# Row statistics of a pair split into an early mean and late squares, a row tile turned earlier, and the last statistics spread over the mixing

## The chip, the cores and the metric

The kernel runs on one core of a Trainium2 chip. A core has five engines that each take their instructions in order and wait for each other through semaphores: TensorE (PE in the profile, its weight loads PEld), VectorE (DVE), ScalarE (ACT), GpSimd (POOL) and SyncE (SP, which only issues DMAs here). ScalarE and GpSimd issue DMAs too, and such an issue stands in the engine's own order. Data lies in HBM, in the core's SBUF, and in eight PSUM banks into which TensorE writes. The metric is the device time of one execution in microseconds.

## The reference

Two layers, each a linear attention block (A) and a gated block (B), on one sequence of 2048 rows of 512 features, in float32:

```python
x = x + A(layernorm(x)); x = x + B(layernorm(x))      # twice

def A(x):      # 32 heads of 16
    q, k, v = split(x @ wqkv)
    pq, pk = phi(q), phi(k)                           # phi(t) = where(t > 0, t + 1, exp(t)) + 1e-6
    kv, z = sum over rows of pk (x) v, sum over rows of pk
    return ((pq @ kv) / (pq @ z + 1e-6)) @ wo

def B(x):
    z = gelu(x @ w_in)                                # 2048 x 1792
    z1, z2 = z[:, :896], layernorm(z[:, 896:])
    g = w_sp @ z2 + b_sp[:, None]                     # w_sp is 2048 x 2048: the mixing
    return (z1 * g) @ w_out
```

The change concerns how `z2`, the normalised second half, is made in the second layer.

## The kernel before, in words

Every float32 product is made of three single-pass products: both factors are split into a high part (`fp32r`, by a copy on ScalarE) and a low part (the difference, by VectorE), and TensorE adds high x high, high x low and low x high. Everything on the small engines serves these splits, the statistics and the passing out of PSUM.

The order is written out by hand: each engine runs its instructions in the order in which the program calls them, and there is no scheduler. SBUF pages, larger tiles (`quads`, `bigs`) and PSUM banks come from lists in which the one that has been free longest is taken first, so a moved call also changes which buffer follows which.

A layer has four stages: `P1` (keys, queries), a transition, `P2` (output of the attention, then both halves of `gelu(x @ w_in)`), and `P4` (mixing, gate and output product). In `P2`, step `s` works on several row tiles of 128 rows at once:

- `b_high(s)`, `b_low(s)`: tile `s` of the attention's numerators, turned by way of DRAM, is transposed in blocks by VectorE (L353) and split on ScalarE and VectorE;
- `a2_den`, `a2_mul`: denominators of tile `s + 2`;
- `c(s-1)`: twelve matmuls (L117 to L119); `c2` adds the result to `x`; `c_stats` takes mean and variance on VectorE (L289, L291) and the inverse root on GpSimd (L293 to L296); `c3` normalises on ScalarE (L302) and stores the tile on SyncE's queue, from which `xturn.load` fetches it back turned once that store has landed;
- `d_high(s-2)`, `d_low(s-2)`: the tile normalised one step before is transposed (L353), its high part made by ScalarE (L103, into a `qd` tile), its low part by VectorE (L106);
- `f()`: one front unit, twelve matmuls for a piece of `z1`, a gelu on ScalarE (L996) and its store, issued on ScalarE's queue (L999).

In the second layer, from step 9 on, `z2` is made for pairs of row tiles. A pair `m` (tiles `2m` and `2m+1`) is a 2 x 2 block matrix that is multiplied by a 2 x 2 block weight with seven block products, P1 to P7, in place of eight (`product`, L805 to L807). They accumulate in PSUM: the bank `X` takes P1, then P6, then P7, then P4; the bank `Z` takes P5, then P3; `y` takes P2. Between them ScalarE copies a bank into the tile of `z` (`copy`, L824) and VectorE adds another one to it (`add`, L819). `block_sums` forms sums of the blocks (L766 to L769), which `parts` splits for P3, P5, P6 and P7 (written into tiles named `z_s` or into pages). A pair lasts three steps: an odd step makes P1 and P2 of pair `m` and P7, P4 and P3 of the pair before (`o`); an even step makes P6 and P5 of pair `m`; the last quarter of pair `m` is added and passed through gelu in the even step of pair `m + 1`.

Each gelu (`gelu`, L814) also leaves the sum of its rows. `row_stats` turns the two sums of a row tile into the negative mean `nm` on GpSimd (L831), takes the sum of squared deviations with two ScalarE instructions (L836, which write into a PSUM bank that nobody reads), and finds `rs` and `nb` on GpSimd (L840 to L843). `e4` then normalises the tile on ScalarE (L302), and for the first eight tiles subtracts two column ranges on VectorE (L975).

The order in an odd step, cut to what matters: `b`, `a2_den`, `c`, P7 and its copy, P1 and its copy, P2, `c2`, `c_stats`, the addition of `Z` to tile `2o+1`'s high half, `a2_mul`, `c3`, two gelus, `f`, `d`, `block_sums`, P4 and its gelu, P3, `parts`, `f`, `e4` of pair `m - 2`. P3 writes into the bank `Z` that the addition reads. In an even step: `b`, last quarter of pair `m - 1`, `a2_den`, `c`, `c2`, `c_stats`, `a2_mul`, `parts`, `f`, `c3`, P6 and a copy, P5, `row_stats` of pair `m - 1`, `d`, `f`.

The mixing `P4` also uses seven products, of 8 steps each; a mixing step `g` is `mm(g)`, 24 matmuls on eight banks (L1239 to L1241), behind `prepare`, which splits weights of step `g + 2` (L1198, L1205) and rows of step `g + 3` (L1203, L1209). Before the loop, the remaining front units run, and `finish` ends the last pair: last quarter, row statistics and normalisation, in one piece.

Of the kernel before, what the change touches and what calls it, by code (L numbers as in the profile page):

```python
# [10 lines left out]
F32 = mybir.dt.float32  # L11
F32R = mybir.dt.float32r
AF = mybir.ActivationFunctionType
OP = mybir.AluOpType

P = 128
S = 2048
D = 512
FH = 896
# [35 lines left out]
def mixer_kernel(ctx: ExitStack, tc: tile.TileContext, x_in, wqkv, wo_d, win1_d, win2_d, wsp_d, bsp_d, wout_d,  # L55
                 ident_d, mask_d, out_d):
    nc = tc.nc
    consts = ctx.enter_context(tc.tile_pool(name="consts", bufs=1))
    main = ctx.enter_context(tc.tile_pool(name="main", bufs=1))
    small = ctx.enter_context(tc.tile_pool(name="small", bufs=4))  # L60
# [70 lines left out]
    class Weight:  # L131


        def __init__(self, slots, shape, pieces, turned=False, keep=None):
            self.slots, self.shape, self.pieces, self.turned, self.keep = slots, shape, pieces, turned, keep
            self.h = self.l = None
            self.raw = deque()
            self.n_load = self.n_split = 0
# [139 lines left out]
    def w_in1():  # L278
        return Weight(bigs, [P, NF, 4, P], [win1_d[f] for f in range(NF)], keep=kept_in1)
# [358 lines left out]
    class P2:  # L638
        def __init__(self, p1):
            self.L = L = p1.L  # L640
            self.p1 = p1
            self.win1, self.win2 = (w_in1() if self.L == 0 else Parts(kept_in1, NCHK, 3)), p1.win2
            self.qturn, self.xturn = Turn(f"qt{L}", range(5), True), Turn(f"yt{L}", range(4))
            self.qp, self.qT, self.x, self.ms, self.xB, self.z, self.zms = {}, {}, {}, {}, {}, {}, {}
            self.fq = deque()
            self.fnext = []
            self.rows = []
            self.S, self.S_pages = [None, None], []
            self.X, self.Z, self.acc = {}, {}, {}
            self.sums2 = None if self.L == 0 else Sums2()  # L650

        def loadx(self, i):
# [170 lines left out]
                ztag(i, [P, FH], f"z{self.L}")  # L823
            nc.scalar.activation(ztile[i][:, s], b, AF.Copy)  # L824

        def row_stats(self, i):

            a, b = self.acc.pop(i)
            k = FH ** -0.5
            nm = small.tile([P, 1], F32, name="nm")  # L830
            nc.gpsimd.tensor_scalar(nm, a, b, -k / FH, op0=OP.add, op1=OP.mult)  # L831
            sq = banks.get([P, HF])
            v = []
            for s in (self.LO, self.HI):
                w = small.tile([P, 1], F32, name="sq", tag=f"sq{s.start}")
                nc.scalar.activation(sq, ztile[i][:, s], AF.Square, bias=nm, scale=k, accum_out=w)  # L836
                v.append(w)
            banks.put(sq)
            rs = small.tile([P, 1], F32, name="rs")
            nc.gpsimd.tensor_scalar(rs, v[0], v[1], LN_EPS, op0=OP.add, op1=OP.add)  # L840
            nc.gpsimd.tensor_tensor(rs, rs, mhalf, op=OP.pow)
            nb = small.tile([P, 1], F32, name="nb")
            nc.gpsimd.tensor_scalar(nb, nm, rs, 1 / k, op0=OP.mult, op1=OP.mult)  # L843
            self.zms[i] = None, rs, nb
# [14 lines left out]
        def odd(self, s):  # L859

            m = (s - 3) // 2
            o = m - 1
            new, old = m < HT, o >= PAIRED
            if s < NT:
                self.b_high(s)
                self.b_low(s)
            self.a2_den(s + 2)
            if s <= NT:
                self.c(s - 1)
            if old:  # L870
                self.product(self.X[o], o, "P7")
                self.copy(2 * o + 1, self.HI, self.X[o])
            if new:
                X, y = banks.get([P, HF]), banks.get([P, HF])
                self.X[m] = X
                self.product(X, m, "P1", start=True)
                self.copy(2 * m, self.LO, X)
                self.product(y, m, "P2", start=True, stop=True)
            if s <= NT:
                self.c2(s - 1)  # L880
                self.c_stats(s - 1)
            if old:
                self.add(2 * o + 1, self.HI, self.Z[o])
            self.a2_mul(s + 2)
            if s <= NT:
                self.c3(s - 1)
                self.xturn.load(s - 1)
            self.a(s + 3)
            if old:
                self.gelu(2 * o + 1, self.HI)  # L890
            if new:
                self.add(2 * m, self.LO, y)
                banks.put(y)
                self.gelu(2 * m, self.LO)
            self.f()
            if new:
                self.d_high(s - 2)
                self.d_low(s - 2)
                self.block_sums(m)
            if old:  # L900
                X = self.X.pop(o)
                self.product(X, o, "P4", stop=True)
                self.gelu(2 * o + 1, self.LO, X)
                banks.put(X)
                self.product(self.Z[o], o, "P3", stop=True)
                pages.put(*self.S_pages)
                self.S_pages = []
            if new:
                self.S[0] = self.parts(self.sraw[0], (2 * m + 1, 2 * m + 2))
            self.f()  # L910
            self.two(self.e4, m - 2)

        def even(self, s):

            m = (s - 4) // 2
            if s < NT:
                self.b_high(s)
                self.b_low(s)
            self.last_quarter(m - 1)
            self.a2_den(s + 2)  # L920
            if s <= NT:
                self.c(s - 1)
                self.c2(s - 1)
                self.c_stats(s - 1)
            self.a2_mul(s + 2)
            self.S[1] = self.parts(self.sraw[1], (2 * m + 5, 2 * m + 6))
            self.f()
            if s <= NT:
                self.c3(s - 1)
                self.xturn.load(s - 1)  # L930
            self.a(s + 3)
            Z = self.Z[m] = banks.get([P, HF])
            self.product(self.X[m], m, "P6")
            self.copy(2 * m, self.HI, self.X[m], False)
            self.product(Z, m, "P5", start=True)
            self.two(self.row_stats, m - 1)
            if s <= NT + 1:
                self.d_high(s - 2)
                self.d_low(s - 2)
            self.f()  # L940

        def finish(self):
            m = HT - 1
            self.last_quarter(m)
            self.two(self.row_stats, m)
            self.two(self.e4, m)

        def e(self, i):
            n, k = divmod(i, 4)
# [187 lines left out]
    class P4:  # L1137
# [203 lines left out]
        def run(self, nxt):  # L1341
            p2 = self.p2
            self.prepare(0, 0)
            self.fetch(2)
            while p2.f():
                pass
            if p2.L == 0:
                p2.win1.free()
            self.prepare(1, 1)
            self.fetch(3)  # L1350
            self.prepare(None, 2)
            if p2.L > 0:
                p2.finish()
            self.gb = [bigs.get([P, NF, 512]) for _ in range(NCHK)]
            n = len(self.steps)
            for g in range(n):
                p, k = self.steps[g]
                self.prepare(g + 2, g + 3)
                self.mm(g)
                self.fetch(g + 4)  # L1360
                if g in (1, 4, 7) or 8 <= g < 28:
                    self.sums.tick()
                if g == 3:
                    self.loadb()
                self.gates()
                if p == "P3":
                    if k < NF:
                        self.wpiece(k)
                    if k == 6:
                        self.loadx(0)  # L1370
                        self.loadx(1)
                    if k == 7:
                        self.zsplit(0)
                if k == HT - 1:
                    self.evac(p)
            pages.put(*self.bs)
            self.zsplit(1)
            make = Make() if nxt is not None else None
            for i in range(NT):
                self.loadx(i + 2)  # L1380
                flush()
                self.gates()
                if make is not None:
                    if i in (0, 4):
                        make.fetch(i // 4)
                    make.split()
                self.o(i)
                self.zsplit(i + 2)
                if make is not None and i >= 1:
                    make.add()  # L1390
                if nxt is not None:
                    self.join(i, nxt)
# [24 lines left out]
    for L in range(2):  # L1417
        p1.run()
        p2 = P2(p1)
# [39 lines left out]
```

## Time and profile before

| | us |
|---|---|
| median of three runs | 1422.91 (1422.43 to 1423.13) |
| the profiled execution's own time | 1422.4 |
| its span in the profile | 1420.6 |
| granted TensorE clock, mean | 0.99 |
| TensorE busy | 1392.9 (98%) |
| VectorE, ScalarE, GpSimd busy | 898.1, 613.3, 450.8 |

The paired steps lie between 914 and 1058 us of the span, the second layer's mixing begins at 1058.07. In the page, a row of part 5 is a group of equal instructions; in the order of time, a row gives start and duration in us, the engine, the line, output and inputs, and in square brackets the idle time before it and what ended it. Matmuls overlap: a matmul of 512 columns lasts 0.39 us in the trace, but the next one starts 0.23 us after it; so PE's work is read from the distance of starts.

### The profile page before, as it was taken

The page shows a single profiled execution, that of the slowest core. Times are in us where ns is not written, and L with a number is a line of the kernel's source. Part 1 is how long each engine was busy: PE and PEld are TensorE (multiplying, and loading weights), DVE is VectorE, ACT ScalarE, POOL GpSimd, SP SyncE. Part 2 cuts the span into 40 slices and gives each one's busy share as a digit, 9 for nine tenths or more (in the row PEclk, how much of TensorE's full clock was granted, in tenths as well). Part 3 has the DMA queues.
Part 4 walks back from the last instruction along what each step waited for, and adds up shares of the span by engine and source line. Part 5 has one row for each costly group of instructions (what it writes and reads, how often), then busy time and mean ns, then how long its engine had stood idle before and what let it go on. Part 6 is the DMA issues. An engine that isn't in the chain of part 4 may idle for free.

```text
span 1420.6 us, 17881 instructions
## 1 busy us (share of the span) xinstructions
PE 1392.9 (98%) x6240; PEld 1162.7 (82%) x6240; DVE 898.1 (63%) x1282; ACT 613.3 (43%) x985; POOL 450.8 (32%) x569
## 2 busy tenths in 40 slices
PE   9999999999999999999999999998889999999998
PEld 7888888888888888888888888786777888888887
DVE  6785788743755687566677677675435345776642
ACT  6775543333343234233476554445555332342420
POOL 3343445443155623331033334533410000223310
PEclk9999999999999999999999999999998999999999
DMA  5541467866688954457645217986653223543542
GB/s 176 161 134 53 149 213 249 262 209 206 195 289 299 296 173 142 164 185 257 246 135 169 69 50 210 289 250 181 212 172 104 97 96 119 178 138 135 186 134 96
DMA packets 157003, 251.42 MB, mean 177 GB/s; under 512 B 13808, under 2 KB 56048, under 8 KB 156912
## 3 DMA queue, kind: packets, MB, share of 16 engines
q1 hardware_dynamic: 143664, 224.57, 48.3%
q0 software_dynamic: 9216, 18.35, 4.6%
q10 hardware_dynamic: 4032, 7.34, 1.4%
q8 instruction: 49, 0.80, 0.2%
q14 instruction: 42, 0.34, 0.1%
HBM read 174.98 MB, written 75.24 MB: 176 GB/s over the span
## 4 chain that ended last, share of the span: by engine, by line
PE 85%; ACT 4%; DVE 4%; DMA 3%; POOL 2%; issue 2%; ACTq 0%; POOLq 0%; DVEq 0%; SPq 0%
PE bank L119 15%; PE bank L117 15%; PE bank L118 15%; PE bank L1239 13%; PE bank L1240 13%; PE bank L1241 13%; DMA yt<-pg 1%; ACT bank L836 1%; DVE st L289 1%; POOL rs L294 1%; ACT z_z L302 1%; ACT pg L302 1%; ACT pg L996 1%; DVE pg L717 0%; DVE pg L106 0%
## 5 line engine op out<-in xcount | busy, mean ns | idle before, releaser
L1239 PE MATMUL bank<-qd,pg 128*128 128x512 f32 x800 | 312.9, 391 | 6.7 <-DVE z_z L819 3.8
L1240 PE MATMUL bank<-qd,pg 128*128 128x512 f32 x800 | 312.3, 390 | 0.0
L1241 PE MATMUL bank<-qd,pg 128*128 128x512 f32 x800 | 312.2, 390 | 0.0
L1205 DVE TENSOR_TENSOR qd<-qd,qd 128x1024 fp32r<-128x1024 f32 x112 | 160.3, 1432 | 158.9 <-ACT qd L1198 158.5
L1198 ACT ACTIVATE qd<-qd 128x1024 fp32r<-128x1024 f32 x112 | 118.6, 1059 | 241.6 <-DMA qd<-s 105.8
L119 PE MATMUL bank<-qd,pg 128*128 128x512 f32 x496 | 194.2, 391 | 0.0
L1239 PEld LDWEIGHTS bank<-qd,pg 128*128 128x128 f32 x800 | 150.7, 188 | 39.8 <-ACT bank L836 4.4
L1241 PEld LDWEIGHTS bank<-qd,pg 128*128 128x128 f32 x800 | 150.8, 189 | 31.5
L1240 PEld LDWEIGHTS bank<-qd,pg 128*128 128x128 f32 x800 | 150.9, 189 | 31.2
L1261 POOL TENSOR_TENSOR bg<-bg,pg 128x512 f32<-128x512 f32 x56 | 80.6, 1443 | 301.9 <-DMA pg<-z 285.7
L117 PE MATMUL bank<-qd,pg 128*128 128x512 f32 x400 | 157.1, 393 | 3.6 <-ACT qd L103 2.8
L118 PE MATMUL bank<-qd,pg 128*128 128x512 f32 x400 | 156.9, 392 | 0.0
L293 POOL TENSOR_SCALAR rs<-mv 128x1 f32<-128x1 f32 x86 | 36.0, 419 | 321.1 <-DVE mv L291 320.9
L1114 POOL TENSOR_TENSOR pg<-pg,pg 128x512 f32<-128x512 f32 x64 | 93.8, 1465 | 89.9 <-DMA pg<-in_wsp_dram 73.2
L302 ACT ACTIVATE pg<-pg,nb,rs 128x512 f32<-128x512 f32 x63 | 51.1, 811 | 148.5 <-POOL nb L296 143.9
L119 PEld LDWEIGHTS bank<-qd,pg 128*128 128x128 f32 x496 | 93.5, 189 | 20.6 <-DVE pg L106 0.9
L103 ACT ACTIVATE pg<-pg 128x512 fp32r<-128x512 f32 (+2 forms) x87 | 53.1, 611 | 108.2 <-DVE pg L353 56.1
L117 PEld LDWEIGHTS bank<-qd,pg 128*128 128x128 f32 x400 | 75.6, 189 | 19.8 <-ACT qd L103 3.2
L118 PEld LDWEIGHTS bank<-qd,pg 128*128 128x128 f32 x400 | 75.6, 189 | 16.1 <-DVE qd L106 0.9
L119 PE MATMUL bank<-wo,qd 128*128 128x512 f32 x224 | 87.2, 389 | 0.0
L118 PE MATMUL bank<-wo,qd 128*128 128x512 f32 x224 | 87.1, 389 | 0.0
L117 PE MATMUL bank<-wo,qd 128*128 128x512 f32 x224 | 87.1, 389 | 0.0
(168 smaller groups left out, 2627.9 us busy)
## 6 DMA issues: line engine op xcount, KB each, us to landing
qd<-s SPq DMA_DIRECT2D x64, 512.0 KB, 3.3
qd<-in_wsp_dram SPq DMA_DIRECT2D x48, 512.0 KB, 4.1
pg<-in_wsp_dram SPq DMA_DIRECT2D x64, 256.0 KB, 5.0
s<-pg SPq DMA_DIRECT2D x64, 256.0 KB, 4.6
pg<-x SPq DMA_DIRECT2D x64, 256.0 KB, 3.3
pg<-z SPq DMA_DIRECT2D x56, 256.0 KB, 3.6
pg<-win POOLq DMA_DIRECT2D x56, 256.0 KB, 4.7
x<-pg SPq DMA_DIRECT2D x48, 256.0 KB, 3.0
```

The costliest lines, as they stand in the source:

```text
L103: nc.scalar.activation(h, src, AF.Copy)
L117: nc.tensor.matmul(out, ah, bh, start=start, stop=False)
L118: nc.tensor.matmul(out, ah, bl, start=False, stop=False)
L119: nc.tensor.matmul(out, al, bh, start=False, stop=stop)
L302: nc.scalar.activation(y, x, AF.Identity, bias=nb, scale=rs)
L1114: nc.gpsimd.tensor_tensor(t, a, b, op=OP.add)
L1198: nc.scalar.activation(w[:, 0], r, AF.Copy)
L1205: nc.vector.tensor_sub(w[:, 1], r, w[:, 0].bitcast(F32))
L1239: m(out, h[:, o], w[:, 0, j, :], start=start, stop=False, skip_group_check=True)
L1240: m(out, h[:, o], w[:, 1, j, :], start=False, stop=False, skip_group_check=True)
L1241: m(out, l[:, o], w[:, 0, j, :], start=False, stop=stop, skip_group_check=True)
L1261: nc.gpsimd.tensor_tensor(u, u, z1, op=OP.mult)
```

## The change

Four things change in the second layer's `P2`, and one in `P4`.

1. `row_stats` is cut into `row_mean` (GpSimd's `nm`) and `row_squares` (the rest). In the even step `row_mean` of both tiles of the pair is called right behind the last quarter's gelu, and `row_squares` at the end of the step, behind `d_high`, `d_low` and the second `f`.
2. In the odd step `d_high` and `d_low` are called ahead of the additions and gelus of the halves and of `f`; before, they came behind them.
3. The addition of `Z` to tile `2o+1`'s high half moves from ahead of `a2_mul` to behind `d_low`.
4. `finish` is cut into three: last quarter and means before the mixing's loop; the squares after the preparation that mixing step 0 makes; the normalisations after that of mixing step 1.

No arithmetic is added or removed; the counts of instructions stay.

```diff
-        def row_stats(self, i):
+        def row_mean(self, i):
             a, b = self.acc.pop(i)
+            nm = self.nm[i] = small.tile([P, 1], F32, name="nm")
+            nc.gpsimd.tensor_scalar(nm, a, b, -FH ** -1.5, op0=OP.add, op1=OP.mult)
+
+        def row_squares(self, i):
+            nm = self.nm.pop(i)
             k = FH ** -0.5
-            nm = small.tile([P, 1], F32, name="nm")
-            nc.gpsimd.tensor_scalar(nm, a, b, -k / FH, op0=OP.add, op1=OP.mult)
             sq = banks.get([P, HF])
...
         def odd(self, s):
...
-            if old:
-                self.add(2 * o + 1, self.HI, self.Z[o])
             self.a2_mul(s + 2)
             if s <= NT:
                 self.c3(s - 1)
                 self.xturn.load(s - 1)
             self.a(s + 3)
+            if new:
+                self.d_high(s - 2)
+                self.d_low(s - 2)
             if old:
+                self.add(2 * o + 1, self.HI, self.Z[o])
                 self.gelu(2 * o + 1, self.HI)
             if new:
                 self.add(2 * m, self.LO, y)
...
             self.f()
             if new:
-                self.d_high(s - 2)
-                self.d_low(s - 2)
                 self.block_sums(m)
...
         def even(self, s):
...
             self.last_quarter(m - 1)
+            self.two(self.row_mean, m - 1)
             self.a2_den(s + 2)
...
             self.product(Z, m, "P5", start=True)
-            self.two(self.row_stats, m - 1)
             if s <= NT + 1:
                 self.d_high(s - 2)
                 self.d_low(s - 2)
             self.f()
-
-        def finish(self):
+            self.two(self.row_squares, m - 1)
+
+        def finish(self, k):
             m = HT - 1
-            self.last_quarter(m)
-            self.two(self.row_stats, m)
-            self.two(self.e4, m)
+            if k == 0:
+                self.last_quarter(m)
+                self.two(self.row_mean, m)
+            elif k == 1:
+                self.two(self.row_squares, m)
+            elif k == 2:
+                self.two(self.e4, m)
...
             if p2.L > 0:
-                p2.finish()
+                p2.finish(0)
...
                 self.prepare(g + 2, g + 3)
+                if p2.L > 0:
+                    p2.finish(g + 1)
                 self.mm(g)
```

More of the change, by code (lines that the diff above doesn't have):

```diff
@@ L648, in __init__ @@
             self.S, self.S_pages = [None, None], []
-            self.X, self.Z, self.acc = {}, {}, {}
+            self.X, self.Z, self.acc, self.nm = {}, {}, {}, {}
             self.sums2 = None if self.L == 0 else Sums2()
```

## The prediction

> **What bounds the kernel now.** I read the page first, then TensorE's waits, then busy time and granted clock by stretch, and last each engine's order of time where TensorE waits.
>
> ```profile
> span 1420.6 us, 17881 instructions
> ...
> PE 1392.9 (98%) x6240; PEld 1162.7 (82%) x6240; DVE 898.1 (63%) x1282; ACT 613.3 (43%) x985; POOL 450.8 (32%) x569
> ...
> L1198 ACT ACTIVATE qd<-qd 128x1024 fp32r<-128x1024 f32 x112 | 118.6, 1059 | 241.6 <-DMA qd<-s 105.8
> ```
>
> TensorE sets the time: it is busy 1392.9 of 1420.6 us. Only its idle time, and what it runs slowly after idling, can be won or lost. Its waits (us in total, times, longest):
>
> ```profile
> PE bank L805 <- ACT qd L103: 10.5, 3, 5.0
> PE bank L1239 <- DVE z_z L819: 3.8, 1, 3.8
> PE bank L1239 <- ACT bank L836: 2.9, 2, 1.7
> ...
> PE bank L805 <- ACT z_z L824: 0.8, 2, 0.5
> ```
>
> All lie in the second layer's gated block: in its paired steps and the first step of its mixing, which are what the change touches. Behind them (busy time and count of PE, PEld, DVE, ACT, POOL, then clock, DMA share, GB/s):
>
> ```profile
> 1076.00:1416.00 340.00, 340.00 (x1502) 281.52 (x1501) 187.56 (x215) 105.74 (x142) 50.12 (x34) 1.00 0.39 132
> ```
>
> From 1076 on PE is never idle, at clock 1.00. Whatever moves the start of the mixing moves the end by as much. PE's order of time, at its waits and at the marks I follow:
>
> ```profile
> 925.05 0.80 PE L117 MATMUL bank<-qd,pg 128*128 128x512 f32 x1 [2.81 <-ACT qd L103]
> ...
> 929.55 0.36 PE L805 MATMUL bank<-bg,z_s 128*128 128x448 f32 x1
> ...
> 938.65 0.37 PE L805 MATMUL bank<-bg,qd 128*128 128x448 f32 x1
> ...
> 941.09 0.39 PE L117 MATMUL bank<-qd,pg 128*128 128x512 f32 x1
> ...
> 943.83 0.36 PE L805 MATMUL bank<-bg,qd 128*128 128x448 f32 x1
> ...
> 945.04 0.37 PE L805 MATMUL bank<-bg,z_s 128*128 128x448 f32 x1
> ...
> 968.71 0.74 PE L805 MATMUL bank<-bg,qd 128*128 128x448 f32 x1 [5.01 <-ACT qd L103]
> ...
> 973.04 0.39 PE L117 MATMUL bank<-qd,pg 128*128 128x512 f32 x1
> ...
> 977.00 0.37 PE L805 MATMUL bank<-bg,z_s 128*128 128x448 f32 x1
> ...
> 997.77 0.74 PE L805 MATMUL bank<-bg,qd 128*128 128x448 f32 x1 [4.08 <-ACT qd L103]
> ...
> 1002.42 0.63 PE L117 MATMUL bank<-qd,pg 128*128 128x512 f32 x1
> ...
> 1006.83 0.37 PE L805 MATMUL bank<-bg,z_s 128*128 128x448 f32 x1
> ...
> 1024.21 0.47 PE L805 MATMUL bank<-bg,qd 128*128 128x448 f32 x1 [1.46 <-ACT qd L103]
> ...
> 1027.07 0.39 PE L117 MATMUL bank<-qd,pg 128*128 128x512 f32 x1
> ...
> 1058.07 0.39 PE L1239 MATMUL bank<-qd,pg 128*128 128x512 f32 x1
> ...
> 1071.66 0.80 PE L1239 MATMUL bank<-qd,pg 128*128 128x512 f32 x1 [1.68 <-ACT bank L836]
> ```
>
> At 968.71, 997.77 and 1024.21 P1 of the odd steps 13, 15 and 17 waits for the high part of the row tile that the even step before turned (`d_high`). At 945.04, 977.00 and 1006.83 P3 starts in steps 11, 13 and 15. The twelve products of P1 and P2 take 941.09 - 938.65 = 2.44, P4's six take 1.21 (943.83 to 945.04; P7, P3 and half of P5 and P6 the same), a front unit (`f`) or `c` with its twelve 2.74 (941.09 to 943.83).
>
> An idle spell costs more than itself. The twelve products after 5.01 idle took 973.04 - 968.71 = 4.33, that is 1.9 more than elsewhere; after 4.08 idle 4.65, 2.2 more; after 1.46 idle 2.86, 0.4 more; after 2.81 idle a unit took 929.55 - 925.05 = 4.50, 1.8 more.
>
> **Even step: squares behind the row tile.** ScalarE in steps 11 to 15:
>
> ```profile
> 946.17 0.82 ACT L302 ACTIVATE pg<-pg,nb,rs 128x512 f32<-128x512 f32 x1 [4.50 <-POOL nb L296]
> 946.89 0.56 ACT L814 ACTIVATE z_z<-z_z 128x448 f32<-128x448 f32 x1
> ...
> 948.01 0.58 ACT L996 ACTIVATE pg<-bank 128x512 f32<-128x512 f32 x1
> ...
> 948.99 0.63 ACT L103 ACTIVATE qd<-pg 128x512 fp32r<-128x512 f32 x1 [0.40 <-ACT pg L996]
> ...
> 961.09 0.52 ACT L824 ACTIVATE z_z<-bank 128x448 f32<-128x448 f32 x1
> 963.25 0.64 ACT L836 ACTIVATE bank<-z_z,nm 128x448 f32<-128x448 f32 x1 [1.64 <-POOL nm L831]
> ...
> 966.58 0.64 ACT L836 ACTIVATE bank<-z_z,nm 128x448 f32<-128x448 f32 x1 [1.78 <-POOL nm L831]
> ...
> 968.04 0.61 ACT L103 ACTIVATE qd<-pg 128x512 fp32r<-128x512 f32 x1
> ...
> 970.43 0.63 ACT L103 ACTIVATE pg<-pg 128x512 fp32r<-128x512 f32 x1 [1.29 <-DVE pg L353]
> ...
> 976.43 0.82 ACT L302 ACTIVATE pg<-pg,nb,rs 128x512 f32<-128x512 f32 x1 [4.50 <-POOL nb L296]
> ...
> 981.43 0.64 ACT L103 ACTIVATE z_s<-pg 128x512 fp32r<-128x512 f32 x1 [1.03 <-DVE pg L767]
> ...
> 990.91 0.81 ACT L302 ACTIVATE pg<-pg,nb,rs 128x512 f32<-128x512 f32 x1 [1.55 <-POOL nb L296]
> ...
> 999.49 0.63 ACT L103 ACTIVATE pg<-pg 128x512 fp32r<-128x512 f32 x1 [1.29 <-DVE pg L353]
> ...
> 1003.76 0.82 ACT L302 ACTIVATE pg<-pg,nb,rs 128x512 f32<-128x512 f32 x1 [2.78 <-POOL nb L296]
> ```
>
> In step 12 the squares and their two waits for a mean hold ScalarE from 961.6 to 968.04; `d_high` comes behind them. In the changed order it follows the copy of 961.09 at once, 6.4 earlier, so the waits of P1 go: 5.01 + 1.9, 4.08 + 2.2 and 1.46 + 0.4. The means, taken right behind the last quarter's gelu, are two GpSimd instructions ahead of the statistics of `c`, for which GpSimd sits waiting then: nothing. The four squares (two took 1.46, 966.58 to 968.04, so 3.0) now run behind the step's last front unit, and the next step's `b_high` (970.43 now) stands behind them on ScalarE; behind that lie on VectorE `b_low`, the addition of `c` and its statistics. GpSimd's `rs` and `nb` of the pair come later, but are wanted one step on by the normalisation of the pair (`e4`): nothing. No DMA issue changes its place in a queue by this, except that the unit's store on ScalarE's queue now precedes the squares, to its advantage.
>
> **Odd step: row tile ahead of the pair sums.** VectorE in step 11:
>
> ```profile
> 944.15 0.59 DVE L819 TENSOR_TENSOR z_z<-z_z,bank 128x448 f32<-128x448 f32 x1
> ...
> 949.66 0.69 DVE L106 TENSOR_TENSOR qd<-pg,qd 128x512 fp32r<-128x512 f32 x1 [2.77 <-ACT qd L103]
> ```
>
> Before, the sum of the high half read Z's bank at 944.15, and P3, which writes into that bank, ran at 945.04 without waiting. Now this addition stands behind `d_low` on VectorE, `d_low` waits for `d_high`, and `d_high` stands behind the normalisation of 946.17 on ScalarE. P3 gets a new wait, and behind P3 on PE stand a front unit and the next `c`. From the start of the normalisation to P3: 0.72 (946.17 to 946.89), then `d_high` to `d_low` 0.67 (948.99 to 949.66), `d_low` 0.69, the addition 0.59: 2.7. Step 9 has no old pair: `d_high` passes a gelu and a unit's pass there and comes about 1.4 earlier, so the wait of 2.81 halves and its slow time nearly goes, 2.3 in all; but the products after it wait for a copy on ScalarE that moves by 0.2 alone, so about half is lost before P3 of step 11, and the rest in its wait.
>
> The marks, step by step:
> - Step 11: normalisation at 945.8 (0.2 earlier from step 9, and 0.2 because the addition of 944.15 is out of the way), plus 2.7: P3 at 948.5, 3.4 later than 945.04. PE has been idle for over 4 us, so slow time is as after 4.08 and 5.01: 2.1. PE is 5.5 late.
> - Step 12: before, P3, unit, `c`, unit, P6 and P5, unit ran from 945.04 without a gap: 1.21 + 2.74 x 4 + 2.44 = 14.6, to 959.6. Now 965.1. From there: the unit's pass and the issue of its store 0.98 (948.01 to 948.99), squares 3.0, `b_high` to normalisation 5.8 (970.43 to 976.43, less 0.2), then 2.7: P3 of step 13 at 977.6, against 977.00 now: 0.6 later. PE's work in between is 2.74 + 1.21 + 2.44 + 2.74 + 1.21 = 10.3, so it idles 2.2. The slow time after 2.2 lies between 0.4 (after 1.46) and 1.8 (after 2.81): I take 1.0.
> - Steps 13 to 15: two gelus, unit and gelu (0.56 x 2 + 0.98 + 0.56 = 2.7) bring the split to 980.3 (981.43 now); from there to the next normalisation as now, 9.5 (to 990.91): 989.8. Then `d_high` (1.3), the unit's pass 0.98, squares 3.0, `b_high` at 995.0, 4.3 to the normalisation (999.49 to 1003.76), 2.7: P3 of step 15 at 1002.0, against 1006.83: 4.8 earlier. Idle about 1.2, slow 0.4: 4.4 left.
> - Step 17: P1's 1.46 + 0.4 gone: 6.3 earlier. This step normalises nothing ahead of `d_high`, so P3's addition is in time. Step 19: P4 waits for a copy behind the late squares, 0.98 + 3.0 + 0.5 against 1.21 + 2.74 of PE's work, about 0.5; the copies cost up to 0.5 now: 6.2 earlier at 1058.07.
> - First mixing step: the sum and the gelu that the means need keep their place, so the wait of 3.8 stays. The four squares run in one piece, without the 1.78 for the second mean, but behind one preparation of weights (1.059 each): the bank that is released for 1071.66 comes 0.8 earlier. The normalisations behind are wanted six mixing steps on: nothing.
>
> Sum: 6.2 + 0.8 = 7.0. The profiled execution took 1422.4 and the runs' median is 1422.91; taken off the median: 1415.9.
>
> What I know least is the slow time: 0.4 after 1.46 idle, 1.8 after 2.81. [...]
>
> **Rivals.**
> - *P3 need not wait.* All of 2.3 + 6.9 + 6.3 + 1.9 + 0.8 = 18.2 would be won: 1404.7. Against it: in the changed order P3's first product waits for this very addition, and the normalisation ahead starts after P3's time of now.
> - *A draw.* The waits of P3 in 13 and 15 pay the full slow time (2.1 for 1.0 and 0.4, 2.8 more), and the turned tile's load, issued only when its store has landed, keeps VectorE for a microsecond or two in one of the steps: 4.8 less gain, 1420.7, or a little more.
> - *Slower: P3's wait costs in every odd step what it costs in step 11.* 3.4 + 2.1 = 5.5 four times is 22.0; saved are 18.2: 1426.7. For it: step 11 has nothing to give back, and normalisation, `d_high`, `d_low` and addition are as long in each step. Against it: PE's own work takes 10.3 of the 12.5 in step 13. It decides once PE idles 4 instead of 2.2 there, that is, if `b_high` behind the squares starts 2 later than I have it.
>
> **How the numbers follow.** About 0.2%, 2.8 us, is what can be told from no change. My chain has 0.55 (1412 to 1420, faster throughout); P3 free 0.07; the draw 0.20; slower 0.18. So faster 0.62, same 0.20, slower 0.18. The range leaves out the free P3 and the upper part of the slower case: 1412 to 1425.5.
>
> **What would show it.** Right: P1 no longer waits for `qd` in steps 13, 15 and 17; P3 (products of `z_s`) waits for the addition instead, over 4 us in step 11, 1 to 3 in 13 and 15, not in 17; the squares stand in one run; the mixing starts near 1052. Wrong: P3 waits 4 us each time; or `d_high` or its transpose waits for a transfer; or P3 starts without a wait.

## The result, and the profile after

The changed kernel takes 1420.47 us (median of 20 runs, 1417.45 to 1423.74) against 1423.54 us of the kernel before beside it (20 runs, 1422.03 to 1425.24): a ratio of 0.9976, interval 0.9969 to 0.9983. It is about 3 us faster. The direction is that of the forecast, the size is less than half of its 7.0 us.

The page of the changed kernel, head and busy times (the profiled execution took 1421.4 us):

```profile
span 1419.6 us, 17868 instructions
...
PE 1391.5 (98%) x6240; PEld 1162.2 (82%) x6240; DVE 899.6 (63%) x1282; ACT 611.8 (43%) x985; POOL 451.7 (32%) x569
```

TensorE's waits in it (total, times, longest; lines behind the edit have moved: L819, L824 and L831 are L819, L824 and L830 now, the squares L840, the front unit's pass and store L1005 and L1008, the mixing's first products L1248):

```profile
PE bank L805 <- DVE z_z L819: 8.7, 4, 4.0
PE bank L1248 <- DVE z_z L819: 3.8, 1, 3.8
PE bank L805 <- ACT z_z L824: 2.9, 2, 2.3
PE bank L117 <- ACT qd L103: 2.6, 1, 2.6
...
PE bank L1248 <- ACT bank L840: 2.1, 1, 2.1
```

The 10.5 us that P1 waited for the turned row are gone; 8.7 us of P3 waiting for the addition stand in their place, four times. That exchange was forecast. A wait of 2.3 us for a copy (L824) is there that nothing in the forecast has. The same waits in TensorE's order of time, with the first product of the mixing:

```profile
926.37 0.72 PE L117 MATMUL bank<-qd,pg 128*128 128x512 f32 x1 [2.57 <-ACT qd L103]
...
941.43 0.47 PE L805 MATMUL bank<-bg,z_s 128*128 128x448 f32 x1 [2.35 <-ACT z_z L824]
...
953.72 0.72 PE L805 MATMUL bank<-bg,z_s 128*128 128x448 f32 x1 [4.04 <-DVE z_z L819]
...
982.47 0.47 PE L805 MATMUL bank<-bg,z_s 128*128 128x448 f32 x1 [2.01 <-DVE z_z L819]
...
1007.00 0.47 PE L805 MATMUL bank<-bg,z_s 128*128 128x448 f32 x1 [2.05 <-DVE z_z L819]
...
1031.60 0.47 PE L805 MATMUL bank<-bg,pg 128*128 128x448 f32 x1 [0.55 <-DVE z_z L819]
...
1058.93 0.39 PE L1248 MATMUL bank<-qd,pg 128*128 128x512 f32 x1
...
1069.90 0.80 PE L1248 MATMUL bank<-qd,pg 128*128 128x512 f32 x1 [2.07 <-ACT bank L840]
```

The mixing starts at 1058.93 in this execution, 0.9 later than in the one shown of before, and from there to the bank of 1069.90 it takes 11.0 us (1058.07 to 1071.66, 13.6, before). Of these 2.6 us, 0.9 is the wait for the squares (2.07 us in one for 1.25 and 1.68 in two); the rest is time of the products themselves, fewer of which fall into the stretch at half clock (6.83 us long, for 10.24 before; the last section counts such stretches).

P3 of step 11 is at 953.72, where the forecast has 948.5. Two things lie ahead of it. One is no matter of the change: in this execution step 9's normalisation ran at 924.98 (922.12 in the kernel before). In steps 7 and 8, where the two kernels have the same order and the same pages, `b_low` waited 3.44 and 1.50 us for a store out of the page that it writes; in the execution shown of before it waited 0.80 us in step 7 and for no store in step 8. VectorE in the changed kernel:

```profile
895.07 0.69 DVE L106 TENSOR_TENSOR pg<-pg,pg 128x512 fp32r<-128x512 f32 x1 [3.44 <-DMA z<-pg]
...
906.88 0.69 DVE L106 TENSOR_TENSOR pg<-pg,pg 128x512 fp32r<-128x512 f32 x1 [1.50 <-DMA z<-pg]
```

The other is new: such a wait in step 10, which the kernel before does not have. ScalarE's order of time in the changed kernel:

```profile
924.98 0.81 ACT L302 ACTIVATE pg<-pg,nb,rs 128x512 f32<-128x512 f32 x1 [4.70 <-POOL nb L296]
...
931.57 0.63 ACT L103 ACTIVATE pg<-pg 128x512 fp32r<-128x512 f32 x1 [1.76 <-DVE pg L353]
...
940.13 0.81 ACT L302 ACTIVATE pg<-pg,nb,rs 128x512 f32<-128x512 f32 x1 [6.92 <-POOL nb L296]
...
951.08 0.81 ACT L302 ACTIVATE pg<-pg,nb,rs 128x512 f32<-128x512 f32 x1 [4.26 <-POOL nb L296]
```

And VectorE with the DMA issues of the same stretch:

```profile
928.78 0.35 ACTq L1008 DMA_DIRECT2D z<-pg  x1
...
934.53 0.69 DVE L106 TENSOR_TENSOR pg<-pg,pg 128x512 fp32r<-128x512 f32 x1 [2.99 <-DMA z<-pg]
```

The view of the DMA issues of that stretch gives that store's time from issue to landing as its last number, 5.7 us:

```profile
z<-pg ACTq DMA_DIRECT2D x1, 256.0 KB, 5.7
```

`b_low` of step 10 could run when its high part is there (931.57 plus about 0.6), but writes into a page that still holds the output of step 9's front unit, whose store was issued at 928.78 and took 5.7 us. It waits 2.99 us for it, 2.3 more than for its high part alone. Everything of step 10 hangs on it: the sums, the statistics, the normalisation at 940.13 (15.2 us behind the last one, 13.1 in the kernel before), the copy of L824 that stands behind this normalisation on ScalarE (P7's 2.35 us), and the next normalisation, on which P3 of step 11 hangs. In the kernel before, step 9's store was issued 1.9 us behind the normalisation and landed 4.2 us later:

```profile
924.00 0.33 ACTq L999 DMA_DIRECT2D z<-pg  x1
```

```profile
z<-pg ACTq DMA_DIRECT2D x1, 256.0 KB, 4.2
```

Now it is issued 3.8 us behind it (924.98 to 928.78), since `d_high` and a gelu that waits for an addition behind `d_low` stand ahead of the unit's pass; and pages are taken from a list in the order in which they came free, so the moved calls also changed which one `b_low` gets. In the trace of the kernel before, the first instruction that waits for this store's semaphore is not `b_low` but ScalarE's split `b_high` of step 10, which gets its page one call earlier. It loses nothing there: the store has landed at 928.2, and the split runs at 928.95, behind the transpose.

In step 12 `d_high` follows the copy of 968.15 at once; the squares do stand in one run, and `b_high` behind them:

```profile
968.57 0.62 ACT L103 ACTIVATE qd<-pg 128x512 fp32r<-128x512 f32 x1
...
971.18 0.64 ACT L840 ACTIVATE bank<-z_z,nm 128x448 f32<-128x448 f32 x1 [0.40 <-ACT pg L1005]
...
974.09 0.61 ACT L103 ACTIVATE pg<-pg 128x512 fp32r<-128x512 f32 x1
```

### The profile page after: what moved, and what is told of

It is laid out like the page before. It is cut to its first block, busy times and chain, and to the rows that moved or that the text cites. A ratio compares the mean times of both kernels' runs of the same rounds, so it can differ in the third digit from the quotient of the medians.

```text
span 1419.6 us, 17868 instructions
## 1 busy us (share of the span) xinstructions
PE 1391.5 (98%) x6240; PEld 1162.2 (82%) x6240; DVE 899.6 (63%) x1282; ACT 611.8 (43%) x985; POOL 451.7 (32%) x569
## 5 line engine op out<-in xcount | busy, mean ns | idle before, releaser
L1248 PE MATMUL bank<-qd,pg 128*128 128x512 f32 x800 | 312.5, 391 | 5.9 <-DVE z_z L819 3.8
L1248 PEld LDWEIGHTS bank<-qd,pg 128*128 128x128 f32 x800 | 150.5, 188 | 38.6 <-DVE z_z L819 4.2
L353 DVE STREAM_TRANSPOSE pg<-pg 128x512 f32<-128x512 f32 x75 | 80.9, 1078 | 14.2 <-DMA pg<-yt 11.4
L119 PE MATMUL bank<-wo,qd 128*128 128x512 f32 x224 | 87.3, 390 | 0.0
L118 PE MATMUL bank<-wo,qd 128*128 128x512 f32 x224 | 87.2, 389 | 0.0
```

The lines of the kernel that those rows point to most:

```text
L118: nc.tensor.matmul(out, ah, bl, start=False, stop=False)
L119: nc.tensor.matmul(out, al, bh, start=False, stop=stop)
L353: nc.vector.transpose(y.rearrange("p c (t m) -> p m c t", m=4), r.rearrange("p (m c j) -> p m c j", m=4, c=4))
L1248: m(out, h[:, o], w[:, 0, j, :], start=start, stop=False, skip_group_check=True)
```

## Experiments

All ratios are to the kernel before, run beside each; 0.1% is 1.4 us. Each kernel ran four or five times, the one with the finish alone eleven times. Gains in us over the kernel before are worked out from the ratios.

**The other page in step 10.** The changed kernel, in `b_low`:

```diff
             b, home, h = self.bpart
+            if self.L == 1 and i == 10:
+                pages.free_list.rotate(-1)
             l = pages.get([P, 4, P], F32R)
```

The rotation puts the first page of the list at its end, so later calls get other pages too.

> The changed kernel, with one edit: the addition of the low part in step 10 writes another page, not the one whose store of step 9's front unit was still under way. Theory A (the missing gain is mostly this page): the wait of 2.99 us of that addition for the store goes, the normalisation of step 10, the copy that P7 waited 2.35 us for and P3 of step 11 come about 3 us earlier, P7's wait in step 11 goes, and the time is about 3 us less than that of the changed kernel (1420.5), 1417.5. Theory B (the gain is missing because P3's waits on the addition cost more than I took, wherever their chain starts): the wait goes, but P3's wait in step 11 or 13 grows by as much, and the time stays at 1420.5 within 0.7.

Measured: 1417.54 us (1416.80 to 1419.85), ratio 0.9956 (0.9943 to 0.9968), against 0.9976 (0.9969 to 0.9983) of the changed kernel: 2.8 us less, and the intervals just do not meet. VectorE's addition of step 10 waits for its high part alone:

```profile
929.76 0.69 DVE L106 TENSOR_TENSOR pg<-pg,pg 128x512 fp32r<-128x512 f32 x1 [0.70 <-ACT pg L103]
```

TensorE in this kernel (lines two higher):

```profile
923.88 0.50 PE L117 MATMUL bank<-qd,pg 128*128 128x512 f32 x1 [1.44 <-ACT qd L103]
...
936.69 0.47 PE L807 MATMUL bank<-bg,z_s 128*128 128x448 f32 x1 [0.76 <-ACT z_z L826]
...
948.80 0.74 PE L807 MATMUL bank<-bg,z_s 128*128 128x448 f32 x1 [3.82 <-DVE z_z L821]
...
978.50 0.47 PE L807 MATMUL bank<-bg,z_s 128*128 128x448 f32 x1 [2.02 <-DVE z_z L821]
...
1003.03 0.47 PE L807 MATMUL bank<-bg,z_s 128*128 128x448 f32 x1 [2.08 <-DVE z_z L821]
...
1053.07 0.39 PE L1250 MATMUL bank<-qd,pg 128*128 128x512 f32 x1
```

These are near the marks that the forecast had: P3 at 948.5, 977.6 and 1002.0, the mixing near 1052; and step 9's wait is half of 2.81, as forecast. Not all of the 4.9 us by which P3 of step 11 is earlier than in the changed kernel are the page: 2.5 lie ahead of it (step 9's normalisation is at 922.50 in this execution, for 924.98 there and 922.12 in the kernel before), 2.3 come from the page (12.9 us from that normalisation to the next, for 15.2). The store still took 5.6 us; nothing is held up by it now. So theory A holds: the page is worth about 2.8 us. In the other three kernels below that turn the row tile early in step 9 and keep the page, the same addition waits 3.2 to 3.5 us for the store.

**The addition early again.** The changed kernel, in the odd step:

```diff
+            if old:
+                self.add(2 * o + 1, self.HI, self.Z[o])
             self.a2_mul(s + 2)
...
             if old:
-                self.add(2 * o + 1, self.HI, self.Z[o])
                 self.gelu(2 * o + 1, self.HI)
```

> The changed kernel, with the addition of the pair's high half put back ahead of the multiplication of the next row, as before the change; the row tile stays ahead of everything else, and the page of step 10 is used as in the changed kernel. Theory A (P3's wait on the addition behind the row tile is the price of the change): P3 of steps 11, 13, 15 and 17 no longer waits (4.04, 2.01, 2.05 and 0.55 us in the changed kernel, with about 3 us of slow products behind them), P1 does not wait either, and the time is 1408 to 1412. Rival (the row tile's chain is late for PE in any case: behind the squares the next tile, the next sums or the copies come too late, so that another wait takes the place of P3's): 1418 to 1421, with waits of 2 us and more on the turned row, on the copies or on a bank of step 12 to 18.

Measured: 1411.82 us (1410.61 to 1412.91), ratio 0.9910 (0.9897 to 0.9924): 8.7 us under the changed kernel by the medians, in the range of theory A and far from the rival. P3's four waits add up to as much, but that equality is chance: half-speed time goes with them (10.24 us of half clock in the paired steps of the changed kernel, 6.83 here), and step 9 and the copies wait 2.5 us more. TensorE's waits of the paired steps:

```profile
PE bank L805 <- ACT z_z L824: 4.9, 3, 2.9
...
PE bank L117 <- ACT qd L103: 3.1, 1, 3.1
```

P3 has no wait for the addition and P1 none for the turned row. The longest wait for a copy, 2.9 us, is the page of step 10 again: `b_low` waits 3.48 us for the store here, and with both repairs (below) this copy is waited for 0.81 us.

**The even step and the finish alone.** The kernel before, with the edits of `row_mean`, `row_squares`, `even` and `finish` from the diff, and the odd step as it was:

```diff
     # odd step, against the changed kernel
+            if old:
+                self.add(2 * o + 1, self.HI, self.Z[o])
             self.a2_mul(s + 2)
...
-            if new:
-                self.d_high(s - 2)
-                self.d_low(s - 2)
             if old:
-                self.add(2 * o + 1, self.HI, self.Z[o])
                 self.gelu(2 * o + 1, self.HI)
...
             if new:
+                self.d_high(s - 2)
+                self.d_low(s - 2)
                 self.block_sums(m)
```

> The kernel before, with only the even step and the first mixing steps changed (means early, squares behind the step's last front unit, finish spread over the mixing); the odd step as before. Theory A (the even step holds all the gain, the odd step's move only takes from it): P1's waits in steps 13, 15 and 17 (5.01, 4.08, 1.46 us, with 4.5 of slow products behind them) go, P3 does not wait, the first mixing step is about 1 us shorter: 1407 to 1411. Rival (the squares, now in one run ahead of the next low-part work, make the next odd step late, so that the row tile of the odd step without its move comes late for P1 of the even step or for the front unit): 1417 to 1421.

Measured: 1411.65 us (1410.91 to 1412.22), ratio 0.9911 (0.9898 to 0.9925), 12.7 us faster than before: a little above the range of theory A, far from the rival. The waits in the paired steps:

```profile
PE bank L117 <- ACT qd L103: 4.9, 2, 4.0
...
PE bank L805 <- ACT z_z L824: 1.4, 2, 0.8
...
PE bank L805 <- DVE z_z L819: 0.3, 1, 0.3
```

All of the change's gain is in this half of it.

**The odd step alone.** The kernel before, with the odd step's edit of the diff (row tile ahead of the addition) and nothing else:

```diff
-            if old:
-                self.add(2 * o + 1, self.HI, self.Z[o])
             self.a2_mul(s + 2)
...
             self.a(s + 3)
+            if new:
+                self.d_high(s - 2)
+                self.d_low(s - 2)
             if old:
+                self.add(2 * o + 1, self.HI, self.Z[o])
                 self.gelu(2 * o + 1, self.HI)
...
             if new:
-                self.d_high(s - 2)
-                self.d_low(s - 2)
                 self.block_sums(m)
```

> The kernel before, with only the odd step changed (row tile ahead of the addition of the pair's high half). Theory A (the odd step's move costs, and nothing in it gains beyond step 9): P3 waits for the addition in steps 11, 13 and 15, 3 to 4 us each, P1's waits in steps 13, 15 and 17 stay at 3 to 5 us: 1428 to 1436, slower than before by 5 or more. Rival (the odd step's move is harmless, P3's wait being time that P1 would have waited one step later): 1421 to 1424.

Measured: 1429.34 us (1428.67 to 1429.88), ratio 1.0035 (1.0022 to 1.0049): 5 us slower than before. Its waits:

```profile
PE bank L805 <- ACT qd L103: 6.3, 3, 3.1
PE bank L805 <- DVE z_z L819: 6.1, 3, 4.0
...
PE bank L805 <- ACT z_z L824: 3.5, 1, 3.5
```

The time is in the range of theory A; most of the waits are shorter than it has them: P3's are 3.99, 1.58 and 0.52 us, P1's 1.71, 3.13 and 1.42. The copy's 3.5 us are the page again, for whose store `b_low` waits 3.46 us here. P1 still waits, though less (6.3 us, 10.5 before), since P3 has held TensorE back already. The halves do not add up: 12.7 faster and 5.0 slower would leave 7.7, both together give 3.4. My reading is that, alone, a part of P3's wait falls into time that P1 would have waited anyway, and that nothing is left to absorb it once the even step is mended; no run tests this by itself.

**The finish alone.** The kernel before, with `row_mean` and `row_squares` called together where `row_stats` was, and `finish` in three parts as in the diff.

```diff
             if p2.L > 0:
-                p2.finish()
+                p2.finish(0)
...
                 self.prepare(g + 2, g + 3)
+                if p2.L > 0:
+                    p2.finish(g + 1)
```

> The kernel before, with only the end changed: last quarter, means, squares and normalisations of the last pair spread over the first mixing steps, everything in the paired steps as before. My theory: the four squares run in one piece without the 1.7 us between the second pair of them, the last bank of the first mixing step comes about 1 us earlier, and that is all: about 1 us faster than before. Rival: the preparation of weights ahead of the squares delays the bank instead: 0.5 us or more slower.

Measured: 1422.99 us (1421.11 to 1424.46, 11 runs), ratio 0.9988 (0.9979 to 0.9997), 1.7 us faster, with 0.4 to 3.0 possible. The interval only just leaves out no change; whether the 0.8 of the forecast or twice that is right, the times do not say. The trace agrees with the forecast's step: the first mixing step waits for the squares once, 1.97 us, where the kernel before waits 1.25 and 1.68, which is 1.0 less.

**Both repairs.** The changed kernel with the early addition and the other page, the two diffs above.

> The changed kernel with both repairs: the addition of the pair's high half ahead of the row tile's chain as in the kernel before, and the other page in step 10. Theory: the two losses add up; the wait of 3.5 us for the store in step 10 goes, with it P7's wait of 2.9 us in step 11 that is left with the first repair alone, and the time is 2 to 3 us under that one's 1411.8: 1409 to 1410. Rival: a wait of the same size comes up later (copies, banks), and it stays at 1411.8 within 0.7.

Measured: 1409.64 us (1408.43 to 1410.62), ratio 0.9893 (0.9878 to 0.9908): 15.2 us faster than before, in the range of the theory. By the medians it is 7.9 us under the kernel with the other page alone, whose interval lies far off, and 2.2 us under the one with the early addition alone, whose interval overlaps its own. So the early addition is worth about 8 to 9 us and the page 2 to 3, whichever is mended first. It is the fastest version of the study. Its waits in the paired steps come to 4.6 us in nine small ones; the largest group:

```profile
PE bank L807 <- ACT z_z L826: 2.8, 3, 1.4
```

**The row tile early in step 9 only.** The kernel with the even step and the finish changed, and in the odd step:

```diff
             self.a(s + 3)
+            if new and not old:
+                self.d_high(s - 2)
+                self.d_low(s - 2)
             if old:
                 self.gelu(2 * o + 1, self.HI)
...
             if new:
-                self.d_high(s - 2)
-                self.d_low(s - 2)
+                if old:
+                    self.d_high(s - 2)
+                    self.d_low(s - 2)
                 self.block_sums(m)
```

and the other page in step 10.

> The kernel before with the even step and the first mixing steps changed, the row tile moved ahead in step 9 alone (where there is no older pair whose addition could be held up), and the other page in step 10. Theory: step 9's wait of 3.95 us on the turned row (with the even-step change alone) shrinks to about 1.5 us with its slow products, the sums of step 10 come about 2 us earlier, and 1 to 3 us of the alone-case's 1411.65 go: 1409 to 1410.5. Rival: step 9's wait is made good again by step 13 (the next steps' waits for the sums and copies set the time), and it stays at 1411.65 within 0.7.

Measured: 1411.18 us (1409.87 to 1414.44), ratio 0.9909 (0.9895 to 0.9922), the same as without either edit (0.9911). Step 9's wait is shorter (1.88 us for 3.95) but nothing comes of it: the rival holds, and so does the forecast's sentence that step 9's gain is lost again on the way to P3.

**The addition early in step 11 only.** The changed kernel, with

```diff
+            if old and s == 11:
+                self.add(2 * o + 1, self.HI, self.Z[o])
             self.a2_mul(s + 2)
...
             if old:
-                self.add(2 * o + 1, self.HI, self.Z[o])
+                if s != 11:
+                    self.add(2 * o + 1, self.HI, self.Z[o])
                 self.gelu(2 * o + 1, self.HI)
```

> The changed kernel, with the addition put back ahead in step 11 alone; steps 13, 15 and 17 as changed, step 10's page too. My chain (each step's P3 hangs on the end of the even step before it, so what step 11 saves is carried all the way): P3's 4.04 us and some 1.6 us of slow products go and nothing takes them back, P3 of steps 13 and 15 waits 2 us as before: 1414 to 1415.5. Rival (what step 11 gains is lost again in the longer waits of steps 13 and 15, so that only taking away all of them helps): 1418 to 1420.5.

Measured: 1416.23 us (1414.71 to 1416.57), ratio 0.9938 (0.9926 to 0.9951): 5.4 us under the changed kernel by the ratios, 4.2 by the medians. The time lies between the ranges of my chain and of the rival: most of what step 11 loses is carried to the end, but the chain is not as rigid as I had it. TensorE in this kernel:

```profile
978.83 0.47 PE L805 MATMUL bank<-bg,z_s 128*128 128x448 f32 x1 [3.71 <-DVE z_z L819]
...
1003.39 0.47 PE L805 MATMUL bank<-bg,z_s 128*128 128x448 f32 x1 [0.53 <-DVE z_z L819]
```

P3 of step 13 comes 3.6 us earlier than in the changed kernel, not 5.6, and waits 3.71 us. In step 12 it is no longer the front unit's products that the squares stand behind, but ScalarE itself (its order of time):

```profile
964.48 0.82 ACT L302 ACTIVATE pg<-pg,nb,rs 128x512 f32<-128x512 f32 x1 [1.71 <-POOL nb L296]
...
966.15 0.58 ACT L1008 ACTIVATE pg<-bank 128x512 f32<-128x512 f32 x1
```

The unit's products ended near 964.6 (P7 of step 13 starts at 967.35, twelve products or 2.74 us behind them), and its pass ran at 966.15, behind the normalisation of 964.48.

## Why the prediction was right in direction and wrong in size

- **P1's waits.** Right: gone in steps 13, 15 and 17, because `d_high` follows the copy at once. The even step and the finish alone measure 12.7 us where the forecast's terms for them (6.9, 6.3, 1.9 and 0.8) come to 15.9; in that execution step 9's wait is 3.95 us for 2.81, a turned row is waited for 0.98 us at 1021.82, where nothing waited before, and the copies take 0.85 and 0.57 us for 0.48 and 0.33: 2.7 us together, most of the difference.
- **P3's new wait.** Right in kind and size: 4.04, 2.01 and 2.05 us in steps 11, 13 and 15 for "over 4" and "1 to 3". From the normalisation (951.08) to P3 of step 11 it took 2.64 us for 2.7; from P3 of step 11 to that of step 13, 28.8 us, for 29.1 forecast (948.5 to 977.6), and on to step 15 24.5 us for 24.4. Step 17 waits 0.55 us, for none.
- **The step that failed** is the costing of step 9: "`d_high` passes a gelu and a unit's pass there and comes about 1.4 earlier, so the wait of 2.81 halves", and the sentence for step 11, "normalisation at 945.8 (0.2 earlier from step 9 ...)". I counted what `d_high` gains by passing the front unit's pass, and not what the unit loses: its store is issued 1.9 us later behind the normalisation. Nor did I ask who takes the stored page next, though a moved call moves every buffer behind it in such a list. The next taker was an addition on the very chain that sets P3 of step 11; it waited 2.99 us. With another page the kernel is 2.8 us faster, and its P3's stand within 1.1 us of my marks. Against the forecast's 7.0, that version gains 6.3 us (4.6 to 8.1), where the changed kernel gains 3.4; the 0.7 us that are still missing are less than the interval.
- **The slow time behind waits.** The sum came out by luck (3.5 us either way), the terms did not: 2.1, 1.0 and 0.4 us forecast for steps 11, 13 and 15, about 1.7, 0.1 and 1.7 found. Interpolating between the length of a wait and its slow time was the wrong model, as the section on the hardware shows. Two of the values it was drawn from were misread: behind 1.46 us the granted clock stayed at 1.00, so the 0.4 there was no slow clock, and behind 4.08 us the half clock lasted until 1003.35, past the twelve products, so more than 2.2 us were lost.
- **The rivals.** P3 without a wait was priced at 18.2 us; with both repairs it is 15.2. The slower case, 3.4 + 2.1 in each odd step, did not come: only step 11 paid fully. The draw's 1420.7 is near the time found, but not by its reasons: it wanted slow time in steps 13 and 15 and a load that keeps VectorE; it was the store of a page that kept VectorE, in step 10.

What the 20 runs' scatter of 6 us (3 us before) comes from was not tried.

## What to carry to other kernels

When a call is moved, list what it pushes back as well as what it passes, above all DMA issues on the same engine, and follow each shared buffer to its next taker: in step 10 a write into a page whose store was still under way waited 2.99 us for the landing. Where two moves are bundled, price each alone: here one half was worth 12.7 us and the other took most of it back, mainly because it put an addition that frees a PSUM bank behind a longer chain (8.7 us came back with that addition alone put back, 2.8 with the page alone). A release that another engine needs should stay ahead of work that merely could be earlier.

## What the runs showed of the hardware

The slow products behind the waits lie in stretches of half clock. Busy time and granted clock (the last three columns are clock, DMA share, GB/s) of the changed kernel, cut at the edges of the clock:

```profile
950.37:953.78 3.41, 0.06 (x1) 1.00 0.75 229
953.78:957.20 3.42, 3.42 (x9) 0.50 1.04 221
...
977.68:981.09 3.41, 2.78 (x13) 1.00 0.44 144
981.09:984.51 3.42, 2.04 (x9) 1.00 0.91 245
...
1001.58:1004.99 3.41, 3.38 (x16) 1.00 0.64 232
1004.99:1008.40 3.41, 1.40 (x7) 1.00 0.82 188
1008.40:1011.81 3.41, 3.41 (x10) 0.50 0.98 289
```

In these traces the granted clock reads 1.00 or 0.50, and 0.50 for 3.41 us or a multiple of it (6.83 behind P1's wait of 5.01 us in the kernel before, 10.24 at the start of its mixing). The edges of an execution lie on one grid: in the kernel before the slow stretches begin at 924.84, 965.80, 996.52 and 1064.79, which are 12, 9 and 20 times 3.413 apart; in the changed kernel at 926.48, 953.78, 1008.40 and 1066.42, 8, 16 and 17 times. Cut on that grid, the traces show the half clock behind stretches in which TensorE idled long in sum. P3's waits in steps 13 and 15 are 2.01 and 2.05 us long; the first is cut by an edge into 0.6 and 1.4 us, and full clock follows; the second lies nearly whole in one stretch (2.0 of 3.41), and the next runs at half clock, 1.7 us of work lost. Over eight of the ten profiled executions (all but those of the finish alone and of step 9 only), from 150 us of the span on, of the stretches at full clock in which TensorE idled more than 0.95 us, all 21 with up to 1.69 us were followed by a full one, all 23 with 1.92 or more by a half one; between 1.70 and 1.80 both occur. Two from the kernel with the odd step alone, in the same view, and the one that follows each:

```profile
894.62:898.03 3.41, 1.71 (x8) 1.00 1.14 357
898.03:901.45 3.42, 3.42 (x10) 0.50 0.73 238
...
935.58:938.99 3.41, 1.71 (x8) 1.00 0.03 9
938.99:942.41 3.42, 1.62 (x8) 1.00 0.80 227
```

So in these executions, behind a stretch at full clock, half clock came only where TensorE had idled 1.70 us of it or more, and always with 1.92 or more. The count says nothing of the first 150 us. Of stretches that were themselves at half clock, one with 0.54 us of idling (1063.49 in the kernel with the other page) was followed by another, one with 0.34 us (952.65 with the odd step alone) was not. The first edge behind 150 us lies between 150.01 and 153.24 us in the eight executions, so the grid stands differently to the work in each; within the changed kernel's, two waits of 2 us cost 0 and 1.7 us beyond themselves, as the edges fell.
